# The FFT stage of an FFT and two-MoE kernel: w2 @ phi in four column groups, a token scale from one mask, and rows of three pairs in one buffer

## The chip, the cores and the metric

The kernel runs on one core of a Trainium2 chip. The metric is device time in microseconds (us) of one execution. Five engines work side by side: TensorE (PE in the profile, its weight loads PEld), VectorE (DVE), ScalarE (ACT), GpSimd (POOL) and SyncE (SP), which here issues DMA transfers.

## The reference

```python
X = np.fft.rfft(x, axis=1)                     # x: 8 x 3072 x 256
y = np.fft.irfft(X * F[None], n=3072, axis=1)  # F: the filters
x = y.reshape(24576, 256)
logits = x @ w_gate                            # first MoE: one expert of 8 per token
expert_idx = np.argmax(logits, axis=1)
...
for e in range(8):
    h = np.maximum(x[mask_e] @ w1[e], 0.0)
    out[mask_e] = gate_w[mask_e, None] * (h @ w2[e])
# second MoE: soft dispatch, 8 experts with 4 slots each
logits = out @ phi                             # phi: 256 x 32
slot_input = softmax_over_tokens(logits).T @ out
slot_out[e] = np.maximum(slot_input[e] @ w1[e], 0.0) @ w2[e]
return softmax_over_slots(logits) @ slot_out
```

## The kernel before

The program has one long FFT phase, up to about 757 us, then the first MoE by tiles of 128 rows to about 1630 us, and a last stage for the second MoE. The change lies wholly in the FFT phase.

The FFT phase merges several streams of steps into one fixed program order. A table of numbers (`SCHED`) gives each step its place, and the instructions of a step go to the engines' queues in that order. The streams are: `s1`, the forward transform over 128 points; `s2`, in three groups of batches, a second transform (product `U`, L363), the filter on VectorE (L380 to L385) with an addition on GpSimd (L388), and the transform back (product `W`, L331); `s3`, the inverse transform with the gate of the first MoE; `setup`, which rounds w1; and `setup2`, which forms w2 @ phi for each expert.

`s3` goes over 96 pairs of token tiles. At step i it does the following, on different pairs:

- `product(i+1)`: the inverse transform of the next pair, an fp32 matmul into PSUM (L440).
- `first(i)`: VectorE takes the largest absolute value per token (L455), holds it above 2^-100 (L457), and makes from its exponent bits a power of two that is the token's scale `r` (L459, a bitwise "and" and "xor" with one mask). Up to two waiting gate operations are put behind L455 and two behind L457 (`side`). ScalarE writes the scaled fp16 high part into `rows` (L462, twice).
- `low(i-1)`: VectorE writes the low part (L468, twice), after which the PSUM bank is free.
- `second(i-2)`: eight transposes on TensorE (L477) and ScalarE's copy `xT` (L478); `third(i-3)`: the gate's logits (L496).
- `flush(2)`: two scatters on GpSimd (L404, an indirect DMA), each of which writes 128 rows to their expert's place in DRAM. Before the first of a pair, VectorE copies the pair's metadata into the tail of its `rows` buffer (L403).

Six pairs make a sub-batch (the last two have three each). The gate of a sub-batch runs on VectorE in small operations of 96 elements per partition (L510 to L563), and its pairs are scattered one per step, each ten steps after its own step. `rows` is a ring of sixteen one-pair buffers, so a pair's high part waits for the two scatters of the pair sixteen before.

`setup2` has eight experts. Each has four matmuls of 32x512 in two column groups into `pw` (L680), ScalarE's copy `wsb` of 64x512 (L683), four transposes of 64 rows (L689) and ScalarE's scaling into `w2p` (L690). The w2 tiles come in loads of 1 MB per expert on SyncE's queue. The largest value of all of `w2p` (L694) ends the phase.

Of the kernel before, what the change touches and what calls it, by code (L numbers as in the profile page):

```python
# [9 lines left out]
F32 = mybir.dt.float32  # L10
F16 = mybir.dt.float16
I32 = mybir.dt.int32
# [42 lines left out]
RB = 16  # L55
MASK_EXP = 0x7F800000
# when each step of a stream is due, in the order that the streams are merged by
# [51 lines left out]
def _constants():  # L109
# [52 lines left out]
    # the inverse that takes real and imaginary rows crosswise  # L162
# [22 lines left out]
def build(ctx, tc, A, out):  # L185
# [26 lines left out]
    # scale 2^k / p with p the power of two at or below v, and the inverse of that  # L212
# [12 lines left out]
    # maximum over partitions of v [128, 1], on every partition (PSUM)  # L225
# [19 lines left out]
    # ------------------------------------------------------------------ FFT, gate, routing  # L245
    def fft_phase(ctx):
# [15 lines left out]
        # PSUM banks of a stream, in turn  # L262
# [12 lines left out]
        # loads run ahead of the arithmetic by the depth of their ring  # L275
# [39 lines left out]
        # filters, one ring of four for all groups; rows that no frequency has stay zero  # L315
        # (in the place of the weights that are written last)
# [82 lines left out]
        def flush(n):  # L399
            for _ in range(min(n, len(scat))):  # L400
                rows, gb, a, dest, t = scat.pop(0)
                if t % 2 == 0:
                    V.tensor_copy(rows[:, :, 512:PITCH].bitcast(I32), cmeta[:, gb, a:a + 2, :])  # L403
                i = G.indirect_dma_start(  # L404
                    out=xd, out_offset=bass.IndirectOffsetOnAxis(ap=dest[:, t:t + 1], axis=0),
                    in_=rows[:, t % 2, :].bitcast(U16), in_offset=None, bounds_check=ROWS - 1, oob_is_err=False,
# [6 lines left out]
        def s3(bp, bt, bm):  # L413
            n = B * NA // 2
            # sub-batches of pairs of tiles, short ones at the end
# [14 lines left out]
            rows, xTs, sub, los, p3s, gq = {}, {}, {}, {}, {}, []  # L430
# [5 lines left out]
            # inverse transform of two tiles of tokens  # L436
# [5 lines left out]
            # scaled by a power of two per token, in two fp16 parts  # L442
            def first(i):
# [8 lines left out]
                rw = rows[i] = st.tile([128, 2, PITCH], F16, tag="rows", name=f"rows{i}", bufs=RB)  # L452
# [3 lines left out]
                side(2)  # L456
                V.tensor_scalar(out=am, in0=am, scalar1=2.0 ** -100, scalar2=None, op0=ALU.max)  # L457
                side(2)
                V.tensor_scalar(out=r[:, s_].bitcast(I32), in0=am.bitcast(I32), scalar1=MASK_EXP, scalar2=MASK_EXP,  # L459
# [20 lines left out]
            # one bank: the logits of this sub-batch and the places of the one before  # L480
# [60 lines left out]
            def gate3(k):  # L541
# [8 lines left out]
                def place():  # L550
                    for t in range(rr):
                        scat.append((rows[start[k] + t // 2], gb, a0 + t, dest, t))
# [672 lines left out]
```

## Time and profile before

| What | Value |
|---|---|
| median of three runs | 1751.54 us (1745.28 to 1753.77) |
| profiled execution, span | 1753.4 us |
| TensorE busy over the span | 1482.1 us, 85% |
| VectorE | 1212.9 us, 69% |
| ScalarE | 794.1 us, 45% |
| GpSimd | 637.4 us, 36% |

The shares are means over stages with different limits: what an edit is worth is read in the stage in which it stands. The profiled execution is one run of the program; its span is taken as its time and lies 1.9 us above the median. In the views, `out<-in` names the tile written and the tiles read, `x` a count, and the times are in us unless marked ns. The granted clock is TensorE's, as a share of its full speed.

### The profile page before, as it was taken

What the parts mean: (1) busy time and instruction counts of PE and PEld (TensorE: products, weight loads), DVE (VectorE), ACT (ScalarE), POOL (GpSimd) and SP (SyncE); (2) the same over time, 40 slices, a digit from 0 to 9 for tenths busy, and PEclk for the clock granted to TensorE, in tenths of its full rate; (3) what the DMA queues carried; (4) which work ended last, traced back from release to release, by engine and by line L of the source; (5) the groups of instructions that cost most, each with busy time, mean ns of one, the idle gap of its engine ahead of it and who ended that gap; (6) DMA issues with size and microseconds to landing.
All of it is one profiled execution on the core that took longest, in us unless ns stands there. A gap on an engine that the chain in (4) does not pass through costs nothing.

```text
span 1753.4 us, 35627 instructions
## 1 busy us (share of the span) xinstructions
PE 1482.1 (85%) x10361; PEld 704.0 (40%) x10361; DVE 1212.9 (69%) x3051; ACT 794.1 (45%) x1816; POOL 637.4 (36%) x877
## 2 busy tenths in 40 slices
PE   6777789888888767559999999999999999998886
PEld 1222234333444334224454444444444444444332
DVE  0377789899999856446777777677767776777234
ACT  3344446555766645324444444444434444444133
POOL 0122234665666554522333333233323333333300
PEclk9888889999999987679999999999999999998899
DMA  8999989987888756459999999999999999999999
GB/s 288 309 311 290 293 272 286 291 267 231 245 254 245 223 193 180 138 126 194 223 214 222 212 206 202 179 199 185 185 174 198 193 192 190 194 189 207 352 322 380
DMA packets 720697, 405.71 MB, mean 231 GB/s; under 512 B 554561, under 2 KB 658896, under 8 KB 720512
## 3 DMA queue, kind: packets, MB, share of 16 engines
q1 hardware_dynamic: 634560, 295.09, 75.4%
q10 hardware_dynamic: 69824, 77.52, 14.5%
q0 software_dynamic: 16128, 30.83, 5.3%
q8 instruction: 93, 1.52, 0.4%
q14 instruction: 92, 0.75, 0.1%
HBM read 164.60 MB, written 105.52 MB: 154 GB/s over the span
## 4 chain that ended last, share of the span: by engine, by line
PE 53%; DVE 16%; DMA 13%; issue 7%; ACT 6%; another core or an unknown queue 2%; ACTq 1%; POOL 1%; SPq 0%; DVEq 0%; POOLq 0%
PE ph L846 24%; PE U L363 3%; PE pg L979 3%; PE pl L869 3%; PE W L331 3%; PE p L440 3%; DMA zd<-zo 2%; DVE h L852 2%; PE p L307 2%; PE pg L983 2%; DMA xt<-in_x 2%; DVE rows L468 2%; DMA out_y<-ot 2%; ACT h L851 2%
## 5 line engine op out<-in xcount | busy, mean ns | idle before, releaser
L846 PE MATMUL ph<-w1s,mxt 128*128 x2364 | 550.5, 383 | 44.5 <-issue 34.4
L846 PEld LDWEIGHTS <-mxt 128*128 128x128 f16 x2364 | 236.7, 102 | 305.2 <-issue 69.3
L852 DVE SCALAR_TENSOR_TENSOR h<-ph,h 128x1024 f16<-128x1024 f32 x199 | 243.4, 1223 | 137.4 <-ACT h L851 114.9
L851 ACT ACTIVATE h<-ph 128x1024 f16<-128x1024 f32 x199 | 203.6, 1023 | 175.6 <-PE ph L846 136.5
L404 POOL DMA_INDIRECT xd<-rows,dest x192 | 189.5, 987 | 161.4 <-ACT xT L478 53.3
L388 POOL TENSOR_TENSOR t<-t,t 112x512 f32<-112x512 f32 x112 | 142.0, 1271 | 252.8 <-DVE t L385 242.0
L915 POOL DMA_INDIRECT cd<-cr,meta x199 | 197.2, 991 | 62.2 <-issue 47.2
L363 PE MATMUL U<-zi,mt 96*128 96x512 f32 x256 | 145.0, 651 | 38.1 <-issue 19.0
L331 PE MATMUL W<-t,mt 112*96 112x512 f32 x288 | 151.9, 620 | 2.8 <-ACT vo L332 2.5
L307 PE MATMUL p<-xt,cs 128*128 128x512 f32 x192 | 118.3, 709 | 22.2 <-DMA xt<-in_x 9.9
L440 PE MATMUL p<-vt,cs 128*128 128x512 f32 x192 | 113.3, 675 | 18.8 <-DVE rows L468 18.8
L869 PE MATMUL pl<-w2c,ht 128*128 128x64 f16 x1592 | 114.3, 190 | 16.3 <-DVE fl L891 11.0
L869 PEld LDWEIGHTS <-ht 128*128 128x128 f16 x1592 | 103.1, 96 | 49.2 <-issue 23.0
L478 ACT COPY xT<-tr 128x1024 f16<-128x1024 f16 x96 | 97.0, 1011 | 38.1 <-remote 26.3
L870 PE MATMUL pl<-w2c,ht 128*128 128x32 f16 x1592 | 111.9, 178 | 0.0
L332 ACT COPY vo<-W 96x512 f32<-96x512 f32 x128 | 74.6, 582 | 77.6 <-PE W L331 51.3
L462 ACT ACTIVATE rows<-p,r 128x256 f16<-128x256 f32 x192 | 80.8, 473 | 63.8 <-DVE r L459 33.7
L870 PEld LDWEIGHTS <-ht 128*128 128x128 f16 x1592 | 95.6, 96 | 20.0 <-issue 1.1
L994 DVE TENSOR_TENSOR acc<-acc,pg 128x512 f32 x149 | 101.6, 682 | 0.7 <-issue 0.2
L380 DVE TENSOR_TENSOR t<-U,w2s 112x512 f32<-112x512 f32 x128 | 87.9, 687 | 17.1 <-PE U L363 7.6
L309 ACT COPY zo<-p 128x512 f32<-128x512 f32 x96 | 56.0, 583 | 92.2 <-PE p L307 45.5
L913 POOL TENSOR_TENSOR cr<-x,cr 128x128 f16<-128x128 f32 x50 | 21.8, 436 | 207.8 <-ACT cr L912 207.8
(242 smaller groups left out, 2184.3 us busy)
## 6 DMA issues: line engine op xcount, KB each, us to landing
mx<-xd ACTq DMA_DIRECT2D x199, 130.0 KB
xt<-in_x SPq DMA_DIRECT2D x96, 256.0 KB
zd<-zo ACTq DMA_DIRECT2D x96, 256.0 KB
zi<-zd SPq DMA_DIRECT2D x128, 192.0 KB
vd<-vo ACTq DMA_DIRECT2D x128, 192.0 KB
vt<-vd SPq DMA_DIRECT2D x96, 256.0 KB
out_y<-ot SPq DMA_DIRECT2D x48, 512.0 KB
w2s<-in_ff SPq DMA_DIRECT2D x93, 96.0 KB
```

The costliest lines, as they stand in the source:

```text
L307: PE.matmul(p, cs1[:, 0:128], xt[:, 2 * m:2 * m + 2, :], start=True, stop=True)
L331: PE.matmul(W, mt[:, 128 + 96 * i:224 + 96 * i], t, start=(i == 0), stop=(i == len(ts) - 1))
L363: PE.matmul(U, mt[0:96, 0:128], zi, start=True, stop=True)
L388: G.tensor_tensor(out=t1, in0=t1, in1=t2, op=ALU.add)
L404: i = G.indirect_dma_start(out=xd, out_offset=bass.IndirectOffsetOnAxis(ap=dest[:, t:t + 1], axis=0), in_=rows[:, t % 2, :].bitcast(U16), ...
L440: PE.matmul(p, cs1[:, 128:256], vt[:, 2 * i % CH:2 * i % CH + 2, :], start=True, stop=True)
L846: PE.matmul(ph[:, hf * 512:hf * 512 + 512], xt[:, 2 * part + k, :], w1s[:, ds(e, 1), k, w, hf * 512:hf * 512 + 512].rearrange("p a f -> p ...
L851: SC.activation(h[:, 0, :], ph, AF.Relu)
L852: V.scalar_tensor_tensor(out=h[:, 1, :], in0=ph, scalar=0.0, in1=h[:, 0, :], op0=ALU.max, op1=ALU.subtract)
L869: PE.matmul(pl2s[g][:, q, :], ht[:, k, :], w[:, k, :], start=(q == 0 and k == 0), stop=False, skip_group_check=True)
L870: PE.matmul(pl2s[g][:, q, 0:NS], ht[:, 8 + k, :], w[:, k, 0:NS], start=False, stop=((q == 3 or t == NT - 1) and k == 7), skip_group_check= ...
L915: i = G.indirect_dma_start(out=cd, out_offset=bass.IndirectOffsetOnAxis(ap=metas[g].bitcast(U32)[:, q, 2:3], axis=0), in_=cr[:, q].rearran ...
```

## The change

Three edits, all in the FFT phase:

1. The token scale. L457, the maximum with 2^-100, goes. L459 uses MASK_EVEN (0x7F000000) in place of MASK_EXP (0x7F800000), so that the scale is a power of two with an even exponent and the inverse of a zero maximum stays finite. The four gate operations that `side` may place all come behind L455.
2. `rows`. A ring of six buffers with three pairs each takes the place of sixteen with one pair. The metadata of three pairs is copied by one VectorE instruction of 128x6x4 elements, at the first and the fourth pair of a sub-batch. The scatters are as many as before, in the same order.
3. w2 @ phi. `pw` is 128x256 in four column groups (eight matmuls of 32x256 per expert for four of 32x512), `wsb` is copied as 128x256, and two transposes of 128 rows take the place of four of 64.

```diff
-RB = 16
+RB = 3
 MASK_EXP = 0x7F800000
+MASK_EVEN = 0x7F000000
...
                 rows, gb, a, dest, t = scat.pop(0)
-                if t % 2 == 0:
-                    V.tensor_copy(rows[:, :, 512:PITCH].bitcast(I32), cmeta[:, gb, a:a + 2, :])
+                m = t % (2 * RB)
+                if m == 0:
+                    V.tensor_copy(rows[:, :, 512:PITCH].bitcast(I32), cmeta[:, gb, a:a + 2 * RB, :])
                 i = G.indirect_dma_start(
                     out=xd, out_offset=bass.IndirectOffsetOnAxis(ap=dest[:, t:t + 1], axis=0),
-                    in_=rows[:, t % 2, :].bitcast(U16), in_offset=None, bounds_check=ROWS - 1, oob_is_err=False,
+                    in_=rows[:, m, :].bitcast(U16), in_offset=None, bounds_check=ROWS - 1, oob_is_err=False,
...
-                rw = rows[i] = st.tile([128, 2, PITCH], F16, tag="rows", name=f"rows{i}", bufs=RB)
+                g, m = divmod(i, RB)
+                if m == 0:
+                    ring[g] = st.tile([128, 2 * RB, PITCH], F16, tag="rows", name=f"rows{g}", bufs=6)
+                rw = rows[i] = ring[g][:, 2 * m:2 * m + 2]
...
-                side(2)
-                V.tensor_scalar(out=am, in0=am, scalar1=2.0 ** -100, scalar2=None, op0=ALU.max)
-                side(2)
-                V.tensor_scalar(out=r[:, s_].bitcast(I32), in0=am.bitcast(I32), scalar1=MASK_EXP, scalar2=MASK_EXP,
+                side(4)
+
+                V.tensor_scalar(out=r[:, s_].bitcast(I32), in0=am.bitcast(I32), scalar1=MASK_EVEN, scalar2=MASK_EVEN,
...
-                pw = ps_w([64, 512], f"pw{e}")
+                pw = ps_w([128, 256], f"pw{e}")
                 for k in range(2):
-                    for hf in range(2):
-                        PE.matmul(pw[32 * hf:32 * hf + 32, :], phi[:, k, :], w[2 * k + hf],
-                                  start=(k == 0), stop=(k == 1), tile_position=(0, 32 * hf), skip_group_check=True)
-                wsb = st.tile([64, 512], F32, tag="t2", name=f"wsb{e}", bufs=2)
+                    for cg in range(4):
+                        wk = w[2 * k + cg // 2]
+                        PE.matmul(pw[32 * cg:32 * cg + 32, :], phi[:, k, :], wk[:, cg % 2 * 256:cg % 2 * 256 + 256],
+                                  start=(k == 0), stop=(k == 1), tile_position=(0, 32 * cg), skip_group_check=True)
+                wsb = st.tile([128, 256], F32, tag="t2", name=f"wsb{e}", bufs=2)
                 SC.copy(wsb, pw)
                 yield from pause(3)
                 if e + 1 < E:
                     get(e + 1)
-                pt = ps_w([128, 4, 2, NS], f"pwt{e}")
-                for j in range(4):
-                    PE.transpose(pt[:, j].rearrange("p g s -> p (g s)"), wsb[:, j * 128:j * 128 + 128], id32[0:64, 0:64])
-                SC.activation(w2p[:, e].rearrange("p (b j) s -> p j b s", b=2), pt, AF.Copy, scale=isw1[:, e:e + 1])
+                pt = ps_w([128, 2, 4, NS], f"pwt{e}")
+                for j in range(2):
+                    PE.transpose(pt[:, j].rearrange("p g s -> p (g s)"), wsb[:, j * 128:j * 128 + 128], id32)
+                SC.activation(w2p[:, e].rearrange("p (b j) s -> p j b s", j=2), pt, AF.Copy, scale=isw1[:, e:e + 1])
```

How the change moves instructions is seen in the program's order on two engines. First VectorE, in the middle of a sub-batch of `s3` where the product `p329` is taken up; `p328` is the pair before, `rows18` to `rows20` are the buffers of pairs that are scattered at these steps, and `t1`, `t2`, `U` belong to `s2`. Before:

```order
L403 COPY rows18_3167<-cmeta_91 128x2x4
L455 TENSOR_REDUCE am4_3768<-p329_4009 128x2
L457 TENSOR_SCALAR am4_3768<-am4_3768 128x2
L459 TENSOR_SCALAR r4_3767<-am4_3768 128x2
L468 SCALAR_TENSOR_TENSOR rows28_4011<-p328_3926,r4_3767,rows28_4011 128x256 x2
L403 COPY rows19_3273<-cmeta_91 128x2x4
L380 TENSOR_TENSOR t1280_4101<-U280_3978,w2s_75 112x512
L384 TENSOR_TENSOR t2280_4102<-U280_3978,w2s_75 64x512
L385 SCALAR_TENSOR_TENSOR t2280_4102<-U280_3978,w2s_75 48x512
L455 TENSOR_REDUCE am5_4116<-p330_4056 128x2
L457 TENSOR_SCALAR am5_4116<-am5_4116 128x2
L459 TENSOR_SCALAR r5_4115<-am5_4116 128x2
```

With the change (its line numbers are four or five higher, and two below L404; `rows6` holds the pairs 18 to 20):

```order
L405 COPY rows6_3132<-cmeta_91 128x6x4
L460 TENSOR_REDUCE am4_3719<-p329_3951 128x2
L463 TENSOR_SCALAR r4_3718<-am4_3719 128x2
L472 SCALAR_TENSOR_TENSOR rows9_3872<-p328_3870,r4_3718,rows9_3872 128x256 x2
L381 TENSOR_TENSOR t1280_4038<-U280_3920,w2s_75 112x512
L385 TENSOR_TENSOR t2280_4039<-U280_3920,w2s_75 64x512
L386 SCALAR_TENSOR_TENSOR t2280_4039<-U280_3920,w2s_75 48x512
L460 TENSOR_REDUCE am5_4053<-p330_3996 128x2
L463 TENSOR_SCALAR r5_4052<-am5_4053 128x2
```

Of this stretch the two maxima and the copies of the second and third pair have gone; all else follows in the order in which it stood.

Next GpSimd, where such scatters are issued, with what each waits for (DMASW: that an earlier scatter has landed; DVE and ACT: VectorE's and ScalarE's work). Before:

```order
L404 DMA xd_68<-rows30_4117,dest5_4702 197760x520 [waits DMASW4_49,DVE_49,Activation_49]
L404 DMA xd_68<-rows30_4117,dest5_4702 197760x520 [waits DMASW5_49,Activation_49]
L404 DMA xd_68<-rows31_4173,dest5_4702 197760x520 [waits DMASW6_49,DVE_49,Activation_49]
L404 DMA xd_68<-rows31_4173,dest5_4702 197760x520 [waits DMASW7_49,Activation_49]
L388 TENSOR_TENSOR t12160_4797<-t12160_4797,t22160_4798 112x512 [waits DVE_49,PE_49]
L404 DMA xd_68<-rows32_4211,dest5_4702 197760x520 [waits DMASW0_49,DVE_49,Activation_49]
L404 DMA xd_68<-rows32_4211,dest5_4702 197760x520 [waits DMASW1_49,Activation_49]
L404 DMA xd_68<-rows33_4276,dest5_4702 197760x520 [waits DMASW2_49,DVE_49,Activation_49]
```

With the change, the same places in the order:

```order
L406 DMA xd_68<-rows10_4054,dest5_4616 197760x520 [waits DMASW4_49,DVE_49,Activation_49]
L406 DMA xd_68<-rows10_4054,dest5_4616 197760x520 [waits DMASW5_49,Activation_49]
L406 DMA xd_68<-rows10_4054,dest5_4616 197760x520 [waits DMASW6_49,Activation_49]
L406 DMA xd_68<-rows10_4054,dest5_4616 197760x520 [waits DMASW7_49,Activation_49]
L389 TENSOR_TENSOR t12160_4706<-t12160_4706,t22160_4707 112x512 [waits DVE_49,PE_49]
L406 DMA xd_68<-rows10_4054,dest5_4616 197760x520 [waits DMASW0_49,Activation_49]
L406 DMA xd_68<-rows10_4054,dest5_4616 197760x520 [waits DMASW1_49,Activation_49]
L406 DMA xd_68<-rows11_4206,dest5_4616 197760x520 [waits DMASW2_49,DVE_49,Activation_49]
```

The scatters stand as before between the additions; a wait for VectorE is left at the first scatter of a buffer of three pairs alone.

## Rows read from the trace of the kernel before

**Rows 1.** Busy time of each engine by stretch, with the granted clock and the DMA share.

```profile
230.00:400.00 170.00, 153.57 (x613) 66.52 (x614) 155.07 (x308) 94.77 (x166) 87.29 (x73) 0.99 0.90 283
400.00:600.00 200.00, 171.45 (x1126) 85.69 (x1125) 189.99 (x519) 130.22 (x231) 122.31 (x116) 0.97 0.80 235
600.00:720.00 120.00, 80.38 (x683) 45.79 (x680) 68.18 (x268) 62.05 (x114) 59.94 (x63) 0.83 0.60 190
```

**Rows 2.** The chain of waits, 400 to 600 us: shares by line, and two of its pieces.

```profile
by line: DVE rows L468 12.5%; DVE am L455 9.4%; DVE t L380 7.3%; DVE am L457 7.1%; PE p L440 6.3%; issue 6.2%; PE U L363 6.1%; PE W L331 6.0%; DVE t L384 4.2%; DVE t L385 4.1%; DVE t L382 3.6%; DVE rows L403 3.4%; PE tr L477 3.0%; DMA zi<-z
...
475.32 1.88 DVE am L457
...
590.53 1.88 DVE am L457
```

**Rows 3.** Groups of instructions by line, 400 to 600 us; the last row 600 to 720 us.

```profile
L440 PE MATMUL p<-vt,cs 128*128 128x512 f32 x92 | 51.2, 639 | 8.0 <-DVE rows L468 8.0
...
L457 DVE TENSOR_SCALAR am<-am 128x2 f32<-128x2 f32 x46 | 18.6, 404 | 1.0
...
L403 DVE COPY rows<-cmeta 128x8 int32<-128x8 int32 x45 | 13.5, 300 | 0.0
...
L459 DVE TENSOR_SCALAR r<-am 128x2 int32<-128x2 int32 x46 | 7.9, 171 | 1.1
...
L515 DVE TENSOR_TENSOR d<-lg,lmax 128x96 f32<-128x96 f32 x8 | 2.0, 248 | 0.0
...
L457 DVE TENSOR_SCALAR am<-am 128x2 f32<-128x2 f32 x30 | 5.5, 182 | 0.7
```

**Rows 4.** VectorE's timeline, 460 to 485 us.

```profile
460.86 0.17 DVE L457 TENSOR_SCALAR am<-am 128x2 f32<-128x2 f32 x1
461.07 0.17 DVE L459 TENSOR_SCALAR r<-am 128x2 int32<-128x2 int32 x1
...
465.99 1.18 DVE L403 COPY rows<-cmeta 128x8 int32<-128x8 int32 x1
467.08 0.68 DVE L380 TENSOR_TENSOR t<-U,w2s 112x512 f32<-112x512 f32 x1
...
470.10 0.16 DVE L403 COPY rows<-cmeta 128x8 int32<-128x8 int32 x1
470.17 0.68 DVE L455 TENSOR_REDUCE am<-p 128x2 f32<-128x512 f32 x1
```

**Rows 5.** The timeline of all engines, 473 to 478 us.

```profile
475.24 1.96 DVE L457 TENSOR_SCALAR am<-am 128x2 f32<-128x2 f32 x1
...
475.89 1.28 POOL L388 TENSOR_TENSOR t<-t,t 112x512 f32<-112x512 f32 x1
```

**Rows 6.** The chain of waits, 600 to 765 us: six of its 25 longest pieces.

```profile
616.29 2.27 PE pw L680 x8
627.66 5.20 issue
...
721.00 2.03 PE pw L680 x4
724.35 5.89 another core or an unknown queue
...
738.32 4.75 PE pw L680 x8
743.67 5.78 another core or an unknown queue
```

**Rows 7.** The timeline in the last stage, at 1638 us.

```profile
1638.63 1.07 PE L1108 MATMUL pi<-w2n,gT 128*32 128x256 f32 x16
```

**Rows 8.** The timeline of all engines, 692 to 706 us.

```profile
694.47 0.98 POOL L404 DMA_INDIRECT xd<-rows,dest  x1 [2.14 <-ACT xT L478]
...
703.46 0.98 POOL L404 DMA_INDIRECT xd<-rows,dest  x1 [0.30 <-issue]
704.63 1.01 ACT L478 COPY xT<-tr 128x1024 f16<-128x1024 f16 x1 [5.36 <-remote]
```

More of the change, by code (lines that the diff above doesn't have):

```diff
@@ L429, in s3 @@
             get = ahead(B * NQ, XV, load, lambda i, j: j == i + 1 or grp_of[i // NQ] == grp_of[j // NQ])
-            rows, xTs, sub, los, p3s, gq = {}, {}, {}, {}, {}, []
+            rows, ring, xTs, sub, los, p3s, gq = {}, {}, {}, {}, {}, {}, []
             def side(n):
@@ L551, in place @@
                     for t in range(rr):
-                        scat.append((rows[start[k] + t // 2], gb, a0 + t, dest, t))
+                        scat.append((ring[(start[k] + t // 2) // RB], gb, a0 + t, dest, t))
                 gq.extend([
```

## The prediction

> **What bounds the kernel now.** I read the windows first. From 230 to 600 us VectorE is busy 345 of 370 us (155.07 and 189.99), and in 400 to 600 us 95% against TensorE's 86% (171.45 of 200) [rows 1]. From 600 us neither is full: VectorE 68.18 and TensorE 80.38 of 120 us, so latency sets that stretch. The chain of waits says the same: between 400 and 600 us its largest items are VectorE lines, among them the maximum with 2^-100 (L457, 7.1%) and the copy of the metadata (L403, 3.4%), while TensorE's three products (L440, L363, L331) have about 6% each [rows 2]. From 600 us the chain holds every `pw` product (L680) and long pieces that belong to no work shown [rows 6]. The change reaches all three places and nothing after 768 us, which is over half of the span of 1753.4 us.
>
> **Stage 400 to 600 us, the maximum that is removed.** L457 stands 46 times, 18.6 us busy, 404 ns on average, though its neighbour L459, with the same operation and the same 128x2 elements, takes 171 ns [rows 3]. A normal one moves the next instruction by 0.21 us (460.86 to 461.07) [rows 4]. So 46 x 0.21 = 9.7 us of VectorE goes for certain, and 18.6 - 46 x 0.17 = 10.8 us is extra, in seven long ones of 1.04 to 1.97 us. The one at 475.24 us lasts 1.96 us and ends at 477.20; GpSimd's addition on L388 ends at 477.16 [rows 5]. I read it as VectorE waiting for GpSimd. L459 follows the maximum and would then come to the same place at the same time, so I leave the 10.8 us in the sum as L459's.
>
> The Trainium skill's page "SBUF — State Buffer", section "Who interferes with whom", says that VectorE's copies and tensor-scalar operations can take a port pair that GpSimd uses too, and that whichever comes second is blocked for the whole of the other's instruction. By that rule L459, also a tensor-scalar, inherits the waits; if they were a property of L457 alone, the sum would be 10.8 us larger. This trace agrees with the rule in the two ends at 477.2 us; that L459 would wait in this place no run here shows.
>
> **The copies.** 45 of them stand in this stage, 13.5 us, 300 ns on average [rows 3]; two of three go, so 30. An ordinary one moves the next instruction by 0.07 us (470.10 to 470.17), a long one by 1.09 us (465.99 to 467.08) [rows 4]. The six long ones, once per sub-batch of six pairs, all stand at the third pair of a sub-batch; copies remain at the first and fourth, so all six go: 6 x 1.09 + 24 x 0.07 = 8.2 us. The next instruction there is L380, whose operand comes from PSUM, and the chain shows no long wait on it, so nothing is inherited. The copies that stay write 24 elements per partition in place of 8: between 0 and, by the difference of L459's 171 ns to the 248 ns of L515, which writes 96 elements [rows 3], 0.08 us each, 1.2 us at most for 15. Ring waits: before, each pair waits for the two scatters of the pair sixteen back; now the first pair of a group waits for all six of the group six back, whose last pair is the same sixteen back, so I cost it at nothing. What covers it is the distance: at two scatters a step, the youngest awaited one was issued six steps before (a pair is scattered ten steps after its own). Were it not covered, ScalarE's L462 would stall, then L468 and, since that frees the PSUM bank, the product L440.
>
> **What of it reaches the end of the stage.** Upper bound: all of VectorE's cut, 9.7 + 8.2 = 17.9 us. By the chain: L457 has 7.1% of 200 = 14.2 us, five of its pieces being long ones of 1.82 to 1.89 us [rows 2]; less 5 x (1.87 - 0.21) = 8.3 us that stay with L459, 5.9 us; the long copies' 6.5 us lie within L403's 3.4% = 6.8 us. Together 12.4 us. Lower bound: TensorE stands idle 28.6 us of the 200, and only 8.0 us of it, ahead of L440, is put down to VectorE's L468 [rows 3]; TensorE could give a quarter of that, 2 us. I take **10 us**, nearer the chain, since VectorE's own idle time in the stage is only 10 us.
>
> **Stage 230 to 400 us.** Twenty of the pairs fall here; 20 x 0.21 + 5 x 0.07 = 4.6 us of VectorE at most, 0 at least, since both engines are near 91% and TensorE's work leads the step. I take **1 us**.
>
> **Stage 600 to 720 us.** Thirty maxima at 182 ns [rows 3] give 6.3 us of VectorE, but it idles 52 us here [rows 1]; 0 to 6, I take **1 us**. The `pw` product matters more: it lies on the chain once per sub-batch, in five pieces of 1.87 to 2.27 us at full clock (10.1 us together; the first and the last are shown) [rows 6]. Now it is eight products of 32x256 in four column groups. The nearest row is L1108 of the last stage, which has just that shape, 32x256 f32 in four column groups: 1.07 us for sixteen matmul records, eight products [rows 7]. So 10.1 - 5 x 1.07 = 4.7 us; bounds 0 (the next wait takes it: the product L440 behind it must wait for VectorE's L468 in any case) and 4.7. I take **4 us**. The copy of 128x256 in place of 64x512, and two transposes in place of four, lie beside other work until the end of the phase.
>
> **Tail, 735 to 757 us.** The chain has one `pw` piece of 4.75 us, at a granted clock of about 0.5 (1.2 GHz) [rows 6], of which 2 x 1.92 us are matmuls. At that level the new form takes twice 1.07; 4.75 - 2.14 = 2.6 us, at least 1.5; I take **2 us**. The last `pw` lies beside the 5.78 us piece behind it and counts nothing.
>
> **Sum.** 1 + 10 + 1 + 4 + 2 = 18 us off the profiled execution's 1753.4 us, 1735.4. That execution is 1.9 us above the median 1751.54, so **1733.5 us**. No change is what lies within 0.5%, 8.8 us, which is also the spread of the three runs shown (1745.28 to 1753.77).
>
> **Rivals.**
>
> *TensorE takes over (same).* From 400 us TensorE is 86% busy and the chain hops to it for L440, L363, L331. If each microsecond that VectorE gives back turns into a wait for these products, the stage yields 2, and the products of 600 us 2, the tail 2: 6 us, 1745.5. For it: in 230 to 400 us both engines are at 90%, and VectorE's cut does nothing there. Against it: VectorE's 10 us of idle time in 400 to 600 us.
>
> *The long waits leave with L457 (faster still).* Then 10.8 us more, of which the chain shows 8.3: 1725. For it: L459 is nowhere long between 400 and 600 us. Against it: it always stands behind a wait that has just ended.
>
> *Fewer long pauses.* In 600 to 765 us the chain has six pauses of 5.20 to 5.89 us (627.66 to 743.67 us; the rows show three of them) with no work behind them [rows 6]. Under another of them lies an unbroken run of scatters, 1.28 us apart, eight from 694.47 to 703.46 us; ScalarE's xT copy, after a pause of 5.36 us, starts at 704.63 us, as the run ends [rows 8]. If such runs cause the pauses and the freed scatters spread out, up to four of the five before 730 us could go: 4 x 5.4 = 21.6 us more, 1712.
>
> *More long pauses (slower).* The same mechanism turned round: two scatters of three no longer wait for a VectorE copy, so runs on GpSimd get longer and come to the seven sub-batches between 400 and 600 us, which have none now. Each new pause costs 5.4 us; from six of them it decides ((18 + 8.8) / 5.4 = 5.0), and seven give 1733.5 + 37.8 = 1771. Against it: GpSimd's order does not change, an addition L388 still breaks the runs there, and the runs that fall under the pauses exist already with all their copies.
>
> **How the numbers follow.** The sum as forecast 0.53; TensorE takes over 0.18; waits leave with L457 0.10; fewer pauses 0.08; more pauses 0.09; 0.02 for a smaller loss that I don't name, counted with the same. Faster by over 0.5%: 0.53 + 0.10 + 0.08 = 0.71; within 0.5%: 0.20; slower: 0.09. The bounds of the sum alone are 1.5 + 2 + 2 = 5.5 us (1746) and 4.6 + 17.9 + 6 + 4.7 + 2.6 = 35.8 us (1716). The range goes from 1715 to 1747: it leaves out most of the fewer pauses (0.07), all of the more pauses (0.09) and 0.02 of the rest.
>
> **What would show it.** VectorE's busy time between 400 us and the end of that stage lower by 14 to 18 us, and the stage (first to last L455 of its 46 pairs) 8 to 12 us shorter; L459's mean there up from 171 to about 400 ns, with long ones that end with L388; no L403 over 1 us; `pw` pieces of about 1.1 us in 600 to 720 us; the xT copies' long pauses as many as before, 5.2 to 5.9 us each. Wrong would be: L459 at 0.17 us (the waits left), TensorE's share in 400 to 600 us unchanged at 86% with a stage as long as before (TensorE took over), or pauses of 5 us before 600 us.

## The result

The changed kernel took 1772.11 us (median of 4 runs, 1765.94 to 1777.59), the kernel before 1748.65 us beside it (4 runs, 1745.28 to 1753.77): a ratio of 1.0138, 95% interval 1.0100 to 1.0177. The prediction was 1733.5 us, 1715 to 1747. The profiled execution spans 1765.4 us, against 1753.4.

In the changed kernel L455, L459, L403, L404, L478 and L680 are L460, L463, L405, L406, L482 and L685. The stages are read off the starts of the reduction (L455, L460), the 21st, 67th and 96th of them, and of the reduction that ends the phase:

| us | before | after | difference, running |
|---|---|---|---|
| pair 20 | 407.4 | 403.0 | -4.4 |
| pair 66 | 600.1 | 599.5 | -0.6 |
| pair 95 | 716.2 | 734.5 | +18.3 |
| L694 (L700 of after) | 755.1 | 773.3 | +18.2 |
| end | 1753.4 | 1765.4 | +12.0 |

The loss lies between pair 66 and pair 95, and most of the 4.4 us won by pair 20 is given back between 400 and 600 us. Of those 4.4 us, 1.8 lie ahead of the first pair (its reduction starts at 235.2 us instead of 237.0), where the change does nothing. The first MoE, which the change leaves alone, took 7 us less in this execution. The windows of after, with their columns as in [rows 1]:

```profile
400.00:600.00 200.00, 168.31 (x1117) 84.27 (x1118) 164.24 (x438) 128.82 (x229) 118.00 (x113) 0.97 0.76 230
600.00:720.00 120.00, 67.99 (x600) 39.77 (x599) 53.09 (x181) 52.12 (x96) 55.31 (x57) 0.72 0.55 177
```

VectorE has 25.8 us less to do between 400 and 600 us than in [rows 1]. Some 4 us of this are six instructions of `s2` that fall outside the window now; from pair 20 to pair 66 it is 22.0 us (182.9 to 160.9), still more than the forecast 14 to 18. Yet the stage is no shorter: VectorE is now idle for 36 of 200 us. TensorE's share fell too, so it did not take over. Three groups by line of after, and one of before (L513, the line that is L517 in after), 400 to 600 us:

```profile
L463 DVE TENSOR_SCALAR r<-am 128x2 int32<-128x2 int32 x46 | 10.1, 220 | 1.0
L405 DVE COPY rows<-cmeta 128x24 int32<-128x24 int32 x15 | 2.6, 172 | 0.0
L517 DVE TENSOR_TENSOR lg<-lg,misc 128x96 f32<-128x96 f32 x8 | 2.0, 253 | 20.3 <-ACT lg L514 10.7 <-ACT xT L482 6.3 <-issue 3.2
```

```profile
L513 DVE TENSOR_TENSOR lg<-lg,misc 128x96 f32<-128x96 f32 x8 | 2.0, 247 | 1.9 <-ACT lg L510 1.9
```

The copies cost what was forecast: 15 of them, none long. L463 has 220 ns on average, 2.2 us more than the 7.9 us of L459 in [rows 3], so the 10.8 us of waits that stood at L457 have mostly gone, not moved to it. What VectorE no longer has to do it now waits for: 20.3 us of idle time stand ahead of L517, the first operation of a sub-batch's gate, where there were 1.9. It needs ScalarE's copy of the logits (L514), which runs right behind the xT copy, and the xT copy waits about 4 us once in each of six sub-batches, 3.95 to 4.01 us between 468 and 591 us. Before, no xT copy waits 3 us in this stage. One of the six:

```profile
484.74 0.99 POOL L406 DMA_INDIRECT xd<-rows,dest  x1 [0.17 <-issue]
...
491.12 1.02 PE L442 MATMUL p<-vt,cs 128*128 128x512 f32 x2
491.17 0.98 POOL L406 DMA_INDIRECT xd<-rows,dest  x1 [0.30 <-issue]
492.17 1.28 POOL L389 TENSOR_TENSOR t<-t,t 112x512 f32<-112x512 f32 x1
493.31 1.01 ACT L482 COPY xT<-tr 128x1024 f16<-128x1024 f16 x1 [3.96 <-PE p L442]
...
494.50 0.26 DVE L517 TENSOR_TENSOR lg<-lg,misc 128x96 f32<-128x96 f32 x1 [3.15 <-ACT xT L482]
```

It falls under six scatters in a row, 484.74 to 491.17 us. Before, at most four follow one another there.

The chain of waits from 600 us on, seven of its 35 longest pieces (start, us, what):

```profile
633.15 5.05 another core or an unknown queue
...
648.50 1.32 PE pw L685 x16
...
656.12 2.97 another core or an unknown queue
...
660.18 6.02 another core or an unknown queue
667.43 3.05 another core or an unknown queue
...
739.27 13.18 another core or an unknown queue
756.49 7.91 another core or an unknown queue
```

`pw` is at 1.32 us instead of about 1.9, as forecast in kind. "Another core or an unknown queue" here, and "remote" below, mean that the profile found no event that ended the wait. Where [rows 6] has one such pause of 5.2 to 5.5 us per sub-batch, there are mostly three now, a long one (5.05 to 6.02 us) between two of about 3 us, and the tail has 13.18 and 7.91 us, though it is as long as before. Six pairs (72 to 78, 78 to 84, 84 to 90) take 27.3 us; before, 23.8. One sub-batch's pauses, in the timeline of all engines:

```profile
653.39 0.98 POOL L406 DMA_INDIRECT xd<-rows,dest  x1 [12.19 <-ACT xT L482]
...
656.07 0.42 PE L694 MATMUL pwt<-c,wsb 128*128 128x128 f32 x2
656.33 1.02 PE L442 MATMUL p<-vt,cs 128*128 128x512 f32 x2
...
659.17 1.01 ACT L482 COPY xT<-tr 128x1024 f16<-128x1024 f16 x1 [3.05 <-remote]
...
660.23 1.01 PE L481 MATMUL tr<-id,rows 128*128 128x128 f16 x8 [2.88 <-issue]
...
661.29 2.05 PE L442 MATMUL p<-vt,cs 128*128 128x512 f32 x2
...
666.23 0.47 ACT L695 ACTIVATE w2p<-pwt,isw 128x256 f32<-128x256 f32 x1 [6.05 <-remote]
...
666.96 0.69 DVE L460 TENSOR_REDUCE am<-p 128x2 f32<-128x512 f32 x1 [8.07 <-remote]
667.51 0.98 POOL L406 DMA_INDIRECT xd<-rows,dest  x1 [0.30 <-issue]
...
670.56 1.01 ACT L482 COPY xT<-tr 128x1024 f16<-128x1024 f16 x1 [3.13 <-remote]
670.64 0.69 DVE L460 TENSOR_REDUCE am<-p 128x2 f32<-128x512 f32 x1 [2.01 <-remote]
...
680.69 0.98 POOL L406 DMA_INDIRECT xd<-rows,dest  x1 [12.20 <-ACT xT L482]
```

GpSimd issues twelve scatters in a row, 1.28 us apart, the last at 667.51 us, and then has nothing to do for 12.20 us. Under this run TensorE's transposes `pwt` are recorded at 656.07 us and the product at 656.33 us, but ScalarE's and VectorE's instructions that wait for them start at 666.23 and 666.96 us, and from 660.2 us to 666.2 us neither ScalarE nor VectorE runs anything. In [rows 8] eight scatters follow one another and the wait of the xT copy is 5.36 us.

In the kernel before the rest of a sub-batch's scatters wait for VectorE's next copy:

```profile
655.88 0.98 POOL L404 DMA_INDIRECT xd<-rows,dest  x1 [0.30 <-issue]
...
658.48 0.69 DVE L455 TENSOR_REDUCE am<-p 128x2 f32<-128x512 f32 x1 [6.68 <-PE misc L496]
...
660.47 0.16 DVE L403 COPY rows<-cmeta 128x8 int32<-128x8 int32 x1
...
661.41 0.98 POOL L404 DMA_INDIRECT xd<-rows,dest  x1 [4.55 <-ACT rows L462]
```

The profile names ScalarE as what ended the 4.55 us, but the scatter starts 0.78 us after the end of the copy, and this distance comes back: between 400 and 720 us GpSimd sat idle for over 0.5 us ahead of 49 scatters, and 48 of them start 0.76 to 0.79 us after the end of a metadata copy. In after there are 13 such scatters, all 0.77 to 0.78 us behind one of the few copies that are left. So the copies did set GpSimd's pace, and a pause that stopped VectorE stopped the copies and with them the scatters.

### The profile page after: what moved, and what is told of

It is laid out like the page before. It is cut to its first block, busy times and chain, and to the rows that moved or that the text cites. A ratio compares the mean times of both kernels' runs of the same rounds, so it can differ in the third digit from the quotient of the medians.

```text
span 1765.4 us, 35553 instructions
## 1 busy us (share of the span) xinstructions
PE 1472.5 (83%) x10409; PEld 703.7 (40%) x10409; DVE 1181.2 (67%) x2891; ACT 793.4 (45%) x1816; POOL 636.0 (36%) x877
## 4 chain that ended last, share of the span: by engine, by line
PE 47%; DVE 6%; issue 5%; ACT 5%; another core or an unknown queue 5%; DMA 4%; ACTq 1%; POOL 0%; SPq 0%; DVEq 0%; POOLq 0%
PE ph L852 25%; PE pg L985 3%; PE pl L875 3%; PE pg L989 2%; PE p L442 2%; DMA out_y<-ot 1%; DVE h L858 1%; PE W L332 1%; PE pl L876 1%; DMA ht<-h 1%; ACT xT L482 1%; ACT h L857 1%; PE tr L481 1%; ACT rows L466 1%
## 5 line engine op out<-in xcount | busy, mean ns | idle before, releaser
L406 POOL DMA_INDIRECT xd<-rows,dest x192 | 188.5, 982 | 172.2 <-ACT xT L482 106.6
L332 PE MATMUL W<-t,mt 112*96 112x512 f32 x288 | 158.4, 644 | 0.8 <-ACT vo L333 0.8
L308 PE MATMUL p<-xt,cs 128*128 128x512 f32 x192 | 114.7, 692 | 20.3 <-DMA xt<-in_x 10.0
L482 ACT COPY xT<-tr 128x1024 f16<-128x1024 f16 x96 | 97.0, 1011 | 66.7 <-remote 33.9
L481 PE MATMUL tr<-id,rows 128*128 128x128 f16 x768 | 64.3, 232 | 74.3 <-ACT xT L482 57.5
L875 PEld LDWEIGHTS <-ht 128*128 128x128 f16 x1592 | 103.3, 97 | 44.8 <-issue 20.7
L481 PEld LDWEIGHTS <-rows 128*128 128x128 f16 x768 | 55.7, 104 | 137.9 <-issue 137.9
L460 DVE TENSOR_REDUCE am<-p 128x2 f32<-128x512 f32 x96 | 65.5, 683 | 59.3 <-remote 41.3
```

Source lines behind the costliest of these rows:

```text
L332: PE.matmul(W, mt[:, 128 + 96 * i:224 + 96 * i], t, start=(i == 0), stop=(i == len(ts) - 1))
L406: i = G.indirect_dma_start(out=xd, out_offset=bass.IndirectOffsetOnAxis(ap=dest[:, t:t + 1], axis=0), in_=rows[:, m, :].bitcast(U16), in_o ...
L481: PE.transpose(pt[:, t, k, :], rows[i][:, t, k * 128:k * 128 + 128], id16)
L875: PE.matmul(pl2s[g][:, q, :], ht[:, k, :], w[:, k, :], start=(q == 0 and k == 0), stop=False, skip_group_check=True)
```

## The experiments

The edits 1 to 3 are those numbered in the section on the change, where their diffs stand; runs without a diff below are combinations of them. The runs went to several chips, and the chip matters: the kernel before took 1761 to 1762 us beside the second, third and fifth job (as beside the result, 1749) and 1667 to 1668 us beside the first and the fourth. In the traces from the latter the pauses after 600 us are absent: no xT copy waits 3 us there, but for one each in e3_w2, e4_copy and q1_noload (3.38 to 4.80 us, ended by TensorE's transposes). I call the two kinds chips with and without pauses. Each of the five chips served one job only, so whether it is the chip or something at that hour is not told apart, and the kernel before was traced on the result's chip alone. Each ratio is to runs of before on the same chip.

| run | kernel | pauses | ratio | interval |
|---|---|---|---|---|
| e1_nomax | edit 1 | no | 0.9947 | 0.9917 to 0.9976 |
| e2_ring | edit 2 | no | 0.9960 | 0.9931 to 0.9990 |
| e3_w2 | edit 3 | no | 1.0001 | 0.9966 to 1.0035 |
| e4_copy | all, copies pair by pair | no | 0.9981 | 0.9944 to 1.0018 |
| a1_all | all | yes | 1.0164 | 1.0105 to 1.0222 |
| e5_max_w2 | edits 1 and 3 | yes | 0.9881 | 0.9808 to 0.9953 |
| e6_max_ring | edits 1 and 2 | yes | 1.0134 | 1.0042 to 1.0225 |
| e7_ring_w2 | edits 2 and 3 | yes | 1.0132 | 1.0054 to 1.0209 |
| r1_pace | as e4_copy | yes | 0.9988 | 0.9952 to 1.0024 |
| r2_early | before, copies early | yes | 1.0148 | 1.0052 to 1.0245 |
| r3_fine | edits 1 and 3, a copy per tile | yes | 0.9857 | 0.9759 to 0.9955 |
| r4_gap | all, a memset behind each scatter | yes | 1.0102 | 1.0063 to 1.0141 |
| q1_noload | all, without w2 loads 2 to 7 | no | 0.9926 | 0.9897 to 0.9956 |
| q3_wait | all, waits for landings | no | 1.0111 | 1.0051 to 1.0171 |
| q5_more | edits 1 and 3, twice the bytes | no | 1.0234 | 1.0171 to 1.0298 |
| e5b | edits 1 and 3 | no | 1.0011 | 0.9980 to 1.0041 |
| q1b_noload | as q1_noload | yes | 1.0143 | 1.0091 to 1.0194 |
| a1b_all | all | yes | 1.0097 | 1.0060 to 1.0134 |

And the stages of profiled executions, one for each run, read as in the first table (pair 20 to 66, pair 66 to 95, pair 95 to the last reduction, us):

| run | pauses | 20 to 66 | 66 to 95 | tail |
|---|---|---|---|---|
| before | yes | 192.7 | 116.1 | 38.9 |
| after (the result) | yes | 196.6 | 134.9 | 38.8 |
| a1_all | yes | 197.9 | 138.4 | 39.1 |
| a1b_all | yes | 195.4 | 137.4 | 39.2 |
| e6_max_ring | yes | 201.4 | 141.4 | 39.1 |
| e7_ring_w2 | yes | 197.5 | 136.6 | 39.2 |
| e5_max_w2 | yes | 189.0 | 113.2 | 36.4 |
| r1_pace | yes | 192.3 | 115.4 | 39.5 |
| r2_early | yes | 195.5 | 143.2 | 38.3 |
| r3_fine | yes | 186.7 | 109.1 | 35.0 |
| r4_gap | yes | 197.3 | 134.1 | 39.3 |
| q1b_noload | yes | 199.7 | 135.3 | 39.2 |
| e1_nomax | no | 188.6 | 77.6 | 20.7 |
| e2_ring | no | 185.1 | 74.8 | 21.8 |
| e3_w2 | no | 191.7 | 75.6 | 16.6 |
| e4_copy | no | 189.4 | 76.6 | 16.1 |
| e5b | no | 189.7 | 74.4 | 16.2 |
| q1_noload | no | 181.0 | 77.0 | 16.4 |

### First job: each edit alone, and the pace restored

e4_copy, against the changed kernel:

```diff
-                if m == 0:
-                    V.tensor_copy(rows[:, :, 512:PITCH].bitcast(I32), cmeta[:, gb, a:a + 2 * RB, :])
+                if m % 2 == 0:
+                    V.tensor_copy(rows[:, m:m + 2, 512:PITCH].bitcast(I32), cmeta[:, gb, a:a + 2, :])
```

> The kernel before with edit 1 alone (no maximum with 2^-100, the even mask, four gate operations behind the reduction). Theory 1: the loss comes from the rows edit, because GpSimd's scatters no longer wait for a VectorE copy per pair, run on without a gap, and TensorE's results reach the other engines late while they run. Then this edit alone gains: 3 to 10 us faster, 1740 to 1746. Theory 2: the loss comes from the missing maximum (VectorE meets GpSimd at another place): 15 us or more slower, 1765 or above.

> The kernel before with edit 2 alone (rows of three pairs in one buffer, one metadata copy per three pairs). Theory 1: all of the loss and more is here: 15 to 35 us slower, 1765 to 1785, with the xT copies' long pauses in 600 to 720 us longer than the 5.4 us of before. Theories 2 and 3: 0 to 8 us faster.

> The kernel before with edit 3 alone (w2 @ phi in four column groups). Theory 1: 0 to 7 us faster, 1742 to 1749, the pw pieces at about 1.1 to 1.4 us. Theory 3: four column groups or full-height transposes cost more than they save, or draw out the pauses: 15 us or more slower.

> The changed kernel with the metadata copied pair by pair again (the ring of three-pair buffers stays). Theory 1: the pace is back, so the long pauses are those of before and edits 1 and 3 show their gain: 5 to 15 us faster than before, 1734 to 1744. If the ring's waits for six scatters at once are the cause (theory 4), it stays slow: 1765 or above.

None of the four is slower, e2_ring least of all: it is 0.4% faster, where theory 1 wanted 15 us or more of loss. Theory 1 missed e4_copy too, which it put at 5 to 15 us faster: 0.9981, no difference clear of noise. Theories 2 and 3 want a loss from edit 1 or edit 3, and neither has one here; together they have none on a chip with pauses either (e5_max_w2, below). The four spans are 1656.6 to 1670.8 us, and the trace of e2_ring shows scatters that follow one another at 1.28 us (from 632 us on, 48 in a row), with no pause of the xT copies beside them:

```profile
612.36 0.98 POOL L405 DMA_INDIRECT xd<-rows,dest  x1 [0.31 <-ACT rows L466]
...
613.36 0.61 PE L481 MATMUL tr<-id,rows 128*128 128x128 f16 x8
...
613.64 0.98 POOL L405 DMA_INDIRECT xd<-rows,dest  x1 [0.30 <-ACT xT L482]
...
614.09 1.01 ACT L482 COPY xT<-tr 128x1024 f16<-128x1024 f16 x1
```

Transposes at 613.36 us, their copy at 614.09. So on such a chip a run of scatters does not hold TensorE's results back, and the loss had to be looked for where the pauses are.

e1_nomax also shows what became of the waits at L457. Its groups by line, 400 to 600 us, and one of the waits in the timeline:

```profile
L404 DVE COPY rows<-cmeta 128x8 int32<-128x8 int32 x49 | 19.4, 397 | 0.0
...
L515 DVE SCALAR_TENSOR_TENSOR ca<-d,c 128x96 f32<-128x96 f32 x8 | 9.1, 1135 | 0.2
L458 DVE TENSOR_SCALAR r<-am 128x2 int32<-128x2 int32 x49 | 8.9, 183 | 1.1
L514 DVE TENSOR_TENSOR d<-lg,lmax 128x96 f32<-128x96 f32 x8 | 4.9, 618 | 0.3
```

```profile
514.80 1.49 DVE L514 TENSOR_TENSOR d<-lg,lmax 128x96 f32<-128x96 f32 x1
...
514.89 1.28 POOL L389 TENSOR_TENSOR t<-t,t 112x512 f32<-112x512 f32 x1
```

L458 (the mask) stays at 183 ns, but the two gate operations that `side` now puts ahead of it take 1135 and 618 ns instead of some 250, and the copies 397 instead of 300 [rows 3]. The one at 514.80 us ends with GpSimd's addition. The wait is for GpSimd, as I had read it; it went to the instructions that now meet the addition. The Trainium skill's page "SBUF — State Buffer", section "Who interferes with whom", has this case too: a VectorE instruction with two SBUF inputs contends with a GpSimd instruction that reads SBUF; both L514 (618 ns) and L515 (1135 ns) have two.

### Second job: the other combinations

> The changed kernel itself again, beside the kernel before on the same chip. The chip of the first four runs took 1668 us for the kernel before, 5% less than the 1749 us beside the result, and its traces have none of the pauses of 5 us between 600 and 720 us. Theory 1a: the loss of the change is those pauses made longer (11 us steps of the xT copies in place of 7.7), and needs a chip on which they occur at all: on a chip with before near 1668 us the change is 0.5 to 1.2% faster, on one with before near 1750 us it is 1 to 2% slower. Theory 5: the loss is in the program itself and the edits hinder each other: slower on any chip.

> Edits 1 and 3 without the rows edit. Theory 1a: faster than before on any chip, 0.3 to 1%; on a chip with pauses they are as long as in the kernel before (5 to 6 us). Theory 5 says nothing for it.

> Edits 1 and 2 without the w2 edit. Theory 1a: on a chip without pauses 0.6 to 1.2% faster than before, on one with pauses 1 to 2% slower. If it needs the w2 edit for the loss (full-height fp32 transposes drawing the pauses out), it is no slower than before on either.

> Edits 2 and 3, the maximum kept. Theory 1a: on a chip without pauses 0.2 to 0.7% faster, on one with pauses 1 to 2% slower, as the rows edit alone makes the scatters run on.

This job met pauses. All three kernels with the rows edit are 1.3 to 1.6% slower, whichever other edit goes with it, and the one without it is 1.2% faster (by its interval, 0.5 to 1.9%). Theory 1a holds, and theory 5 and the rival that the loss needs the w2 edit fall: the rows edit is the loss. That it is one on chips with pauses alone rests on e2_ring (0.9960) and later on q1_noload (0.9926); the whole change itself was not timed on a chip without pauses.

The traces of this and the later jobs show the waits of 4 us before 600 us again: the xT copy waits five or six times, 3.01 to 4.06 us each, between 470 and 600 us, in all six further traces from chips with pauses that have the rows edit and two copies per sub-batch (a1_all, a1b_all, e6_max_ring, e7_ring_w2, r4_gap, q1b_noload). In e5_max_w2, r1_pace and r3_fine, which keep the pace, and in r2_early, no xT copy waits 3 us there.

### Third job: pace or ring

r2_early, against the kernel before; and r3_fine, against edits 1 and 3:

```diff
-                if t % 2 == 0:
-                    V.tensor_copy(rows[:, :, 512:PITCH].bitcast(I32), cmeta[:, gb, a:a + 2, :])
+                if t % 6 == 0:
+                    for q in (0, 2, 4):
+                        rq = rows if q == 0 else scat[q - 1][0]
+                        V.tensor_copy(rq[:, :, 512:PITCH].bitcast(I32), cmeta[:, gb, a + q:a + q + 2, :])
```

```diff
-                if t % 2 == 0:
-                    V.tensor_copy(rows[:, :, 512:PITCH].bitcast(I32), cmeta[:, gb, a:a + 2, :])
+                V.tensor_copy(rows[:, t % 2, 512:PITCH].bitcast(I32), cmeta[:, gb, a, :])
...
                     first(i)
+                    flush(1)
...
-                flush(2 if i < n else 12)
+                flush(1 if i < n else 12)
```

r4_gap adds `G.memset(gapt, 0.0)`, a tile of 128x1, behind each scatter of the changed kernel.

> The changed kernel with the metadata copied pair by pair, the ring of three-pair buffers kept (as run e4_copy; this time for a chip with pauses, where before takes 1745 to 1765 us). Theory 1b, pace: in the kernel before, the copy of each pair held its two scatters back to VectorE's step; without it GpSimd runs on, and the pauses grow. Then on a chip with pauses this is 0.5 to 1.5% faster than before, like edits 1 and 3 alone (0.988). Theory 4, ring: the wait for six scatters at once is what costs; then 1 to 1.7% slower, like the whole change (1.016). On a chip without pauses: 0 to 0.8% faster by both.

> The kernel before, with none of the three edits, but the copies of three pairs all issued at the first of them (VectorE's work and the ring of sixteen are those of before). Theory 1b: on a chip with pauses 0.8 to 2% slower than before, with xT steps of 9 to 11 us per sub-batch after 600 us, as with the rows edit. Theory 4: within 0.3% of before. On a chip without pauses within 0.5% by both.

> Edits 1 and 3, and a finer pace: one copy per tile (half as long), one scatter behind the first half of a step and one behind the second, in place of two together. Theory 1b: on a chip with pauses no slower than edits 1 and 3 (0.988), and if the length of a run without a gap is what counts, faster: 0.975 to 0.985, with fewer pauses over 5 us. If the pauses come from elsewhere: as edits 1 and 3, plus up to 4 us for 96 more copies.

> The changed kernel with a memset of 128x1 on GpSimd behind each scatter: the scatters stay unpaced, but no two follow each other directly. If it is the unbroken run of scatter instructions that holds TensorE's results back, the pauses shrink on a chip with pauses and the time falls to 1.000 to 1.008 of before or below. If it is how many scatters are on their way (their transfers), the change stays at 1.013 to 1.02.

r2_early decides between pace and ring. It has none of the three edits, the same VectorE instructions and the same ring of sixteen; only the second and third pair's copies come earlier, and it is 1.5% slower. After 600 us its scatters go twelve in a row, as in after (in before at most eight up to pair 95), and its chain has the pauses of the changed kernel:

```profile
641.75 6.04 another core or an unknown queue
...
669.94 7.53 another core or an unknown queue
```

Before 600 us its runs are of four scatters, as in before, and the waits of 4 us are not there. That stage is 2.8 us longer in the trace all the same; its mask operations are longer there (see the account of L459 below).

r1_pace, with the ring and the pace, is not slower than before: theory 4 falls. But theory 1b put it at 0.5 to 1.5% faster, and it does not reach the 0.988 of e5_max_w2 (their intervals touch at 0.995, on two chips); what the ring costs beside its pace is open. r3_fine, where each tile's scatter waits for a copy of its own, needs 109.1 us for pairs 66 to 95 instead of 116.1, and its pauses of over 4 us are two in that stretch:

```profile
640.61 4.12 another core or an unknown queue
...
661.62 6.87 issue
```

Where GpSimd must wait only twice in a sub-batch, the stretch takes 134.1 to 143.2 us (eight executions); for six copies at VectorE's pace, 113.2 to 116.1 (three); for twelve, 109.1 (one): an order that goes one way. The ratio of r3_fine, 0.9857, can't be told from the 0.9881 of e5_max_w2.

r4_gap has 1.0102 against 1.0164 and 1.0097 of the whole change, between its two forecasts, and its pairs 66 to 95 take 134.1 us, as in after. Its memset takes 0.12 us within the 0.30 us between two scatters, which stay 1.28 us apart: that no other instruction stands between them is not it, but whether a thinner run would help it does not say.

### Fourth and fifth job: what draws the results out

q1_noload leaves out six of the eight w2 loads (the products of experts 2 to 7 are made from other tiles); q3_wait has GpSimd wait for the scatter two before; q5_more adds a plain transfer of the same size behind each scatter of edits 1 and 3:

```diff
+                if e >= 2:
+                    return kept[e % 2]
                 w0 = st.tile([128, F], F32, tag="wt", name=f"wu{e}", bufs=2)
```

```diff
                 order(i)
+                sent.append(rows[:, m, PITCH - 1:PITCH])
+                if len(sent) > 2:
+                    G.memset(sent.pop(0), 0.0)
```

```diff
                 order(i)
+                k = more[0]
+                more[0] += 1
+                SC.dma_start(junk[128 * k:128 * k + 128, :], zrow.bitcast(U16))
```

> The changed kernel without the w2 loads of experts 2 to 7 (their products are made from the tiles of experts 0 and 1 again; 6 of 8 MB are left out). Open: what draws TensorE's results out while the scatters run. Theory A, instructions: GpSimd's scatters, always ready, are enough. Then on a chip with pauses the xT steps of 9 to 11 us after 600 us stay, and the time is within 6 us of the whole change (1.01 to 1.016 of before). Theory B, transfers: the 1 MB loads that meet the scatters are the cause. Then the pauses after 600 us go, and it is 1 to 2% faster than before (0.98 to 0.99), though those between 430 and 600 us stay.

> The changed kernel, and on GpSimd behind each scatter a memset of one column of the rows sent two scatters earlier, which must first have landed. GpSimd then has to wait somewhere between the scatters, for a transfer, not for VectorE. Theory A (a pause ends as soon as GpSimd comes to an instruction that must wait): on a chip with pauses faster than the whole change, 0.985 to 1.003 of before, xT steps after 600 us below 8 us. Otherwise: as run r4_gap, 1.01, or slower still, since a sub-batch's twelve scatters take over 20 us.

> Edits 1 and 3 with the pace of the kernel before (a copy per pair), and one more plain transfer of 128x520 (133 KB, from a constant, to a DRAM buffer that nobody reads) on ScalarE's queue behind each scatter: twice the scatters' bytes with as many GpSimd instructions. Theory A: within 0.5% of edits 1 and 3 alone (run e5b in the same job). Theory B: 1 to 2.5% slower than those, with pauses as in the whole change.

> Edits 1 and 3 again, to set the others against on the same chip: on a chip with pauses 0.985 to 0.995 of before; on one without 0.990 to 0.998.

> Again the changed kernel without the w2 loads of experts 2 to 7, hoping for a chip with pauses (its first run met one without: 0.993). On a chip with pauses, theory A (GpSimd's scatters, always ready, are enough): 1.008 to 1.018 of before, the xT steps of 9 to 11 us after 600 us stay. Theory B (the loads): 0.98 to 0.99, and they go. On a chip without: 0.990 to 0.996.

> The whole change again, beside run q1b_noload. On a chip with pauses 1.012 to 1.018 of before. On one without pauses it has not been timed: the rows edit and the maximum alone gave 0.995 to 0.996 there, so 0.990 to 0.999.

The fourth job met a chip without pauses, so q3_wait and q5_more say nothing on what makes them; they only show that both have a price there (1.1% for the waits, 2.2% for the bytes against e5b). The fifth met pauses, and q1b_noload has them without the loads, 1.0143 beside 1.0097 of the whole change:

```profile
643.25 5.79 another core or an unknown queue
...
670.59 6.78 another core or an unknown queue
```

The w2 loads of experts 2 to 7 are not needed for them. Whether it is GpSimd's instructions or the scatters' own transfers is not told apart by any run.

e5b, edits 1 and 3 on a chip without pauses, gains nothing (0.990 to 0.998 was expected). The chains of e1_nomax and of e5b say why edit 3 adds nothing there: first e1_nomax, then e5b.

```profile
689.35 2.30 DVE v L693
...
703.45 2.44 DMA xd<-rows,dest
...
711.11 4.85 PE ph L845 x12
```

```profile
683.95 2.21 DVE v L695
...
704.37 2.44 DMA xd<-rows,dest
...
711.94 5.29 PE ph L847 x12
```

Edit 3 brings the last reduction 5.4 us forward, but the first product of the MoE (`ph`) starts at 711 to 712 us in both: on a chip without pauses the last scatters, which land at 706 to 707 us, and the load behind them set the start, and the w2 product lies beside them. Why e5b lacks the 0.5% of e1_nomax as well is open.

## Why the prediction was wrong

**The step that failed** is the paragraph on the copies. It priced a copy as VectorE's work, 8.2 us, and put its other role at nothing: in the program's order each pair's two scatters waited for it, and that held GpSimd to VectorE's steps. The order shown ahead of the prediction has these waits, and what follows from their absence was in the text, as the rival of more pauses, with 9 in 100. r2_early shows that moving the copies alone costs 1.5%; e5_max_w2 shows that without this edit the rest gains 1.2% on a chip with pauses, no less than the 1.0% (18 us) that the sum gave for all three.

**The rival was right in mechanism and wrong in its parts.** I counted new pauses of 5.4 us in the seven sub-batches before 600 us, and none longer after it. Before 600 us there came six waits of 4.0 us, which took the 10 us that VectorE had given and 3.9 us more; after it each sub-batch's pauses grew, 27.3 us per six pairs for 23.8, which I had not counted. That its total, 1771 us, lies 1 us from the measured 1772.1 is luck. The arguments against it were true and did not bear: the order is the same, the additions still break the runs and runs of eight were there before, but before 600 us the runs grew from four to six, and after it from eight to twelve.

**The sum, term by term.** In the trace the phase ends 18.2 us later, not 18 earlier; the parts (less is a gain) are -1.8 ahead of pair 0, -2.7 to pair 20, +3.9 to pair 66, +18.9 to pair 95 and -0.1 in the tail.

- *To pair 20*: 2.7 us gained (170.4 to 167.7) for 1.
- *Pair 20 to 66*: forecast a gain of 10, measured a loss of 3.9. VectorE's cut was 22.0 us, not 17.9, because most of the 10.8 us of waits did not go to L463 or elsewhere. The gain of 10 us is there on a chip without pauses: 181.0 us with all three edits (q1_noload, whose missing loads fall behind this stage) against 191.7 with edit 3 alone (e3_w2), one execution each.
- *Pair 66 to 95*: the `pw` pieces measured 1.31 to 1.36 us, and one of 1.86, where 1.07 was taken from L1108. The granted clock was 0.73 to 0.76 in the four pieces and 0.50 (1.2 GHz) in the fifth; each stands behind a pause in which TensorE had little to do (ahead of the third, 0.50 from 669 to 675 us). Nor were the five pieces of before all at full clock: 0.82, 0.99, 0.97, 0.92 and 0.50. At a granted clock of 1.00 the new products take about 1.1 us, as in e5b:

```profile
661.25 0.64 PE L680 MATMUL pw<-wu,phi 128*32 128x256 f32 x8
661.70 0.61 PE L680 MATMUL pw<-wv,phi 128*32 128x256 f32 x8
```

  What the pieces gave to the stretch can't be read: it takes 74.4 to 77.6 us on chips without pauses, with edit 3 or without it, and the pauses hide it on the others.
- *Tail*: on chips without pauses 16.1 to 16.6 us with edit 3, 20.7 and 21.8 without, 4.1 to 5.7 us for 2 forecast; in the result 0.1 us, as the pauses fill the tail.

**L459's inheritance** was half right. That the mask operation waits when it meets GpSimd's addition is shown by r2_early, where it (there L461) takes up to 1.99 us and 408 ns on average; the one at 510.96 us ends at 512.94 us, the addition at 512.90. In e1_nomax the waits go to the instructions that meet the addition there, two gate operations and the copies. In after they are gone almost entirely, but not by the edits: q1_noload, the whole change but for six loads, has them in those two gate operations on a chip without pauses (970 and 522 ns on average between 400 and 600 us; after 256 and 257). In after these operations come some 3 us later, behind the wait for the xT copy, and no longer meet the addition; that this is the reason is read from the rows, not tested.

## What to carry to other kernels

A small copy that a queue of DMA issues waits for is also that queue's pace. Before merging such copies, ask what the queue does when it need not wait, and what runs beside it. A rival that the rows already show at work (runs of eight scatters under the pauses) deserves to be worked out for longer runs, not only for more of them. And a change whose effect hangs on pauses that one chip has and another has not should be timed on both: the same rows edit was 0.4% faster on one and made the loss on the others.

## What the runs showed of the hardware

The kernel before took 1667 to 1668 us on some chips and 1749 to 1762 us on others. The traces show where such a difference lies, if e1_nomax (1664.4 us, with edit 1) is set against before (1753.4 us): the first product of the MoE starts at 711.1 us against 767.2, and the MoE's products take 805 us against 837.

On chips with pauses the instructions that wait for TensorE start up to 10 us after TensorE's own record, while GpSimd runs scatters that find nothing to wait for. Runs of four scatters have no wait of 3 us of the xT copy beside them (before, 400 to 600 us), runs of six have one of about 4 us (after, in the same stage), and runs of eight and twelve after 600 us pauses of over 5 us (before and after); on chips without pauses runs of 48 have none. In the pause shown above the xT copy (670.56 us) and VectorE's reduction (670.64 us) start within 0.08 us of each other, although the transposes that the one waits for are recorded at 660.23 to 661.24 us and the product that the other waits for at 661.29 to 663.34 us. That looks as if the results had long been there and only their signals came late, and together; it is argued from these rows, and no experiment shows it. Why some chips have it is open.
